# Moving one group's key and query transposes from TensorE to the DMA crossbar, with earlier loads and scores

## The chip, the cores and the metric

The kernel runs on one core of a Trainium2 chip. The metric is the device time of one execution in microseconds (us). The core has five engines that run their own instruction streams side by side: TensorE (PE in the profile; its weight loads are PEld), VectorE (DVE), ScalarE (ACT), GpSimd (POOL) and SyncE (SP). SyncE and GpSimd also issue DMA transfers, which sixteen DMA engines carry out.

## The reference

Sliding-window attention with sink tokens, then a gated feed-forward block:

```python
def _attn_ref(q, k, v, n_sink, window):          # q, k, v: (4, 8, 768, 64) float32
    scores = scale * np.matmul(q, k.transpose(0, 1, 3, 2))
    keep = is_sink | in_window                   # n_sink = 4, window = 128
    scores = np.where(keep, scores, -1000000000.0)
    a = softmax(scores)
    return np.matmul(a, v)

def _moe_ref(x, w_gate, w_val, w_out):           # x: (3072, 512), d_ff = 1536
    g = x @ w_gate
    return (g * sigmoid(g) * (x @ w_val)) @ w_out
```

The attention output of 4 batches, 768 positions, 8 heads of 64 becomes x with 3072 rows of 512.

## The kernel before

**Groups and token blocks.** Attention works on 12 groups of 256 positions, three for each batch; group 3 is the first group of batch 1, group 4 the second. The feed-forward part works on eight token blocks of 256, 256, 256, 512, 512, 512, 512 and 256 tokens. Block 2 is fed by group 2, block 3 by groups 3 and 4.

**One group's chain.** The rows of k and q are loaded (`load_nat`, line 106, four loads of 128 KB, issued by GpSimd and cast to bf16 on the way). They have to be turned so that the head dimension lies on partitions. There are two ways in the code: `step_TN` (line 273) does it on TensorE, four matmuls against an identity for each of four tiles, with an eviction from PSUM (L283 or L285) after each tile; `xbar` (line 287) has SyncE issue four DMA transposes that pass the crossbar, straight from the loaded rows to kT and qT, with no work for a compute engine. Then come the scores (`step_S1`, L382, six PSUM banks; three exponentials on ScalarE at L395), three more exponentials (`step_S2`), masks on VectorE at L404 (`step_S2`, `step_S3`), four steps of probabilities times values (`step_PV`, L494, normalized at L503 and L511), and two steps that turn the output into feed-forward input (`step_X`; from group 3 on a DMA transpose on SyncE, L538).

**Order.** The schedule is written out by hand; each engine executes its instructions in program order. The attention work is woven into a list of feed-forward units (`weave`, line 719): a slot `(14, steps)` puts the steps into unit 14. In the first list, units 12 to 17 are the gates of token block 2 (each two projections, pg and pv, 16 matmuls of 256 columns); units 18 to 23 are `down` units, 12 matmuls of 512 columns each, for blocks 0, 1 and 2. In a gate unit a step marked `ahead` (as `S1` is) runs before the gate's first projection, the others between the two projections. In a down unit with n steps they are spread evenly over the 12 matmuls. A second list follows with block 3, whose first unit holds the scores of group 5.

**Banks.** All PSUM tiles come from one pool of eight banks in rotation; scores take six of them.

**Queues.** GpSimd issues the weight loads (`load_gate`, `load_out`) and the k, q and v loads in program order. The order of loads before the first list is written at lines 803 to 814: gates, group 2's rows, more gates, then four parts of the output weights (384 KB each in bf16), then group 3's rows and values. After these GpSimd clears the tile `vcl` (line 815) and SyncE loads the sink values into it (`load_sinks`, eight small loads, L211). All rows from group 4 on share a single buffer (`natp`), so the rows of the next group are loaded only when the crossbar has read the previous ones. `behind` and `turned` (lines 701 and 705) are one-element copies that make GpSimd wait for a transpose.

Of the kernel before, what the change touches and what calls it, by code (L numbers as in the profile page):

```python
# [14 lines left out]
def kernel(  # L15
# [90 lines left out]
    def load_nat(g):  # L106
        b, c = divmod(g, GC)
        x = (natp if g > 3 else rowp).tile(
            [P, 2, 2, DM], BF16, tag="nat" if g > 3 else "rows", name="nat")
        for i, src in ((0, k), (1, q)):  # L110
            for j in range(2):
                t0 = c * 256 + j * P
                nc.gpsimd.dma_start(  # L113
                    x[:, i, j].rearrange("p (h d) -> p h d", d=D),
                    src[b, :, t0:t0 + P].rearrange("h p d -> p h d"))
        nats[g] = x
# [3 lines left out]
    def load_vm(g):  # L120

        b, c = divmod(g, GC)
        if b not in vms:
            vms[b] = vpool.tile([P, 6, H, VS], BF16, tag=f"vm{b}", name="vm")
            nc.gpsimd.memset(vms[b][:, :, :, D:D + 1], 1.0)

        def part(t, p0, p1, t0):
            nc.gpsimd.dma_start(  # L128
                vms[b][p0:p1, t - 1, :, 0:D],
                v[b, :, t0:t0 + p1 - p0].rearrange("h p d -> p h d"))  # L130

        T = 2 * c
        if g - 1 not in QG:
            part(T - 1, 0, 64, P * (T - 1))
            part(T, 0, P, P * T - 64)
        part(T + 1, 0, 64, P * (T + 1))
        part(T + 1, 64, P, P * (T + 1) - 64)
        if c == GC - 1:
            part(T + 2, 0, 64, P * (T + 2) - 64)
        else:  # L140
            part(T + 2, 0, P, P * (T + 2) - 64)

    def load_v(g):
        if g in QG:
            return load_vm(g)
        b, c = divmod(g, GC)
        va = vpool.tile([P, 2, H, VS], BF16, tag=f"va{g}", name="va")
        nc.vector.memset(va[:, :, :, D:D + 1], 1.0)
        for j in range(2):
            t0 = c * 256 + j * P  # L150
            nc.gpsimd.dma_start(  # L151
                va[:, j, :, 0:D], v[b, :, t0:t0 + P].rearrange("h p d -> p h d"))
        vas[g] = va
# [3 lines left out]
    def load_gate(i, which=(0, 1)):  # L157
        f0, n = sum(FCH[:i]) * P, FCH[i] * P
        both = (wgs, moe_w_gate, "wg"), (wvs, moe_w_val, "wv")
        for lst, w, nm in (both[x] for x in which):  # L160
            t = wpool.tile([P, DMC, n], BF16, tag=f"{nm}{i}", name=nm)
            nc.gpsimd.dma_start(
                t, w[:, f0:f0 + n].rearrange("(c p) f -> p c f", p=P))
            lst.append(t)

    def load_out(i):
        n = DFC // 4
        t = wpool.tile([P, n, DM], BF16, tag=f"wo{i}", name="wo")
        nc.gpsimd.dma_start(
            t, moe_w_out[i * n * P:(i + 1) * n * P].rearrange("(c p) f -> p c f", p=P))  # L170
        wos.append(t)
# [12 lines left out]
    one = const.tile([P, 1], FP32)  # L184
# [62 lines left out]
    def new_T(b):  # L247
        if b not in kTs:
            kTs[b] = kqtp.tile([P, NP2, S], BF16, tag="kT", name="kT")
            qTs[b] = kqtp.tile([P, NP2, S], BF16, tag="qT", name="qT")  # L250
# [36 lines left out]
    def xbar(g, which=(0, 1)):  # L287
        b, c = divmod(g, GC)
        new_T(b)
        for i in which:  # L290
            for j in range(2):
                t0 = c * 256 + j * P
                nc.sync.dma_start_transpose(
                    (kTs, qTs)[i][b][:, :, t0:t0 + P], nats[g][:, i, j])
# [378 lines left out]
    def A(fn, *a):  # L673
        return lambda: fn(*a)

    def TN(g, evict="av"):
        return [A(step_TN, g, i, j, evict) for j in range(2) for i in range(2)]
# [4 lines left out]
    def S1(g, apart=False):  # L682
        f = A(step_S1, g, apart)
        f.ahead = True
        return f

    def one(at, g, apart=False):
        return [(at, [S1(g, apart), A(step_S2, g, apart)]), (at + 1, [A(step_S3, g)])]
# [6 lines left out]
    def PVs(g):  # L695
        return [A(step_PV, g, j, hh) for hh in range(2) for j in range(2)]

    def Xs(g):
        return [A(step_X, g, j) for j in range(2)]
# [108 lines left out]
    load_v(2)  # L808
    load_gate(4)
    load_gate(5)  # L810
    for i in range(4):
        load_out(i)
    load_nat(3)
    load_v(3)
    nc.gpsimd.memset(vcl, 0.0)
    nc.gpsimd.memset(vcl[:, :, D:D + 1], 1.0)
    load_sinks(vcl, 1, B)
# [33 lines left out]
    def L(*fs):  # L851
        def f():
            for x in fs:
                x()
        return f

    def NV(g):
        return L(A(load_nat, g), A(load_v, g))
# [3 lines left out]
        ((8, 8), PVs(2)[:2]), (9, [A(step_PV, 2, 0, 1, "a"), A(step_PV, 2, 1, 1, "a")]),  # L862
        ((10, 11), [A(step_X, 2, 0, "a"), ahead(A(step_X, 2, 1, "a"))]),
        (11, [NV(4), lambda: nc.gpsimd.tensor_copy(out=vcl[64:128], in_=vcl[0:64])]),
        ((14, 14, 15, 15), TN(3, "aa")),
        (15, [A(xbar, 4)]), (15, [A(load_nat, 5)]), (19, [A(xbar, 5, (0,))]),
        *one(17, 3), (18, [A(step_ks, 1)]), (18, [A(step_vsb, 1)]),
        ((19, 19, 19, 20), PVs(3)), (19, [S1(4)]), (20, [L(A(step_S2, 4), A(step_S3, 4))]), (20, Xs(3)), (20, [A(xbar, 5, (1,))]),
        ((21, 21, 21, 22), PVs(4)), (21, Xs(4)[:1]),
        (22, [Xs(4)[1], flush, A(behind, 3, 511), A(load_v, 5), A(load_nat, 6)]),  # L870
        (23, [A(xbar, 6), A(turned, 6), A(load_v, 6), NV(7)])))

    def pair(ga, gb, at=0):
# [51 lines left out]
```

## Time and profile before

| What | Value |
|---|---|
| Median of 3 runs | 233.2 us (233.0 to 233.44) |
| Profiled execution | 233.82 us |
| Its span, first to last instruction | 231.9 us |
| Mean granted TensorE clock | 0.993 |
| VectorE, ScalarE, GpSimd busy | 65%, 46%, 36% |
| Loads on the GpSimd queue (q0) | 79904 packets, 14.29 MB |
| SyncE queue (q1) | 30672 packets, 11.58 MB |

The DMA traffic in 40 slices of the span, as busy tenths of the DMA engines:

```profile
DMA  8999999999998998998989996989915102000132
```

The page lists for each engine how long it was busy, and for each group of instructions how many there were, how long one took, and what ended the engine's idle time before them. TensorE's busy time counts pipelined matmuls whose ends are modelled, so the starts of instructions are the better measure of its pace. The tile view of a DMA issue tells how long it took from issue to landing. The DMA view of a time window counts the packets that each queue moved in it.

### The profile page before, as it was taken

The numbers are of one execution on the slowest core, as the hardware profiler recorded it, in microseconds if no ns is written. First come the engines' busy times: TensorE is split into PE (matmuls) and PEld (weight loads), VectorE is DVE, ScalarE is ACT, GpSimd is POOL, SyncE is SP. The second block draws the span as 40 slices with busy tenths as digits, with TensorE's granted clock in tenths as the row PEclk, the third lists the DMA queues.
The fourth block names the chain that finished last, engine by engine and source line by source line (L and its number), as shares of the span: only waits on it lengthen the run. The fifth ranks groups of instructions, "written<-read, shape, count | busy, mean of one in ns | idle before, by whom it ended". The sixth has DMA issues, their size and how long they took to land.

```text
span 231.9 us, 5433 instructions
## 1 busy us (share of the span) xinstructions
PE 225.6 (97%) x2155; PEld 125.4 (54%) x2155; DVE 150.9 (65%) x327; ACT 106.4 (46%) x212; POOL 84.3 (36%) x123
## 2 busy tenths in 40 slices
PE   7699999999999999999999999999999999999994
PEld 3469645796555644455444454454454544487443
DVE  5878888767660797960797970597960599778000
ACT  4784486566543726423635512835612823333221
POOL 8996874960500907806353415135000000000000
PEclk9979999999999999999999999999999999999999
DMA  8999999999998998998989996989915102000132
GB/s 147 150 185 179 179 198 206 164 156 122 123 154 230 103 134 99 151 195 141 146 119 139 128 124 138 105 109 144 117 40 144 45 3 42 3 3 0 64 120 90
DMA packets 112008, 28.04 MB, mean 121 GB/s; under 512 B 99056, under 2 KB 109040, under 8 KB 111984
## 3 DMA queue, kind: packets, MB, share of 16 engines
q0 software_dynamic: 79904, 14.29, 80.7%
q1 hardware_dynamic: 30672, 11.58, 26.7%
q10 hardware_dynamic: 1408, 1.84, 2.5%
q8 instruction: 17, 0.28, 0.5%
q14 instruction: 7, 0.06, 0.1%
HBM read 29.13 MB, written 6.29 MB: 153 GB/s over the span
## 4 chain that ended last, share of the span: by engine, by line
PE 94%; DMA 2%; POOL 2%; DVE 0%; issue 0%; POOLq 0%
PE pg L564 27%; PE pv L564 27%; PE pd L657 27%; PE o L494 4%; PE s L382 3%; DMA rows<-in_q_dram 2%; PE s L326 1%; PE o L463 1%; PE pk L432 1%; PE pn L279 1%; PE o L454 1%; POOL rows L102 1%; POOL x L216 1%; PE px L543 1%; DVE xT L550 0%
## 5 line engine op out<-in xcount | busy, mean ns | idle before, releaser
L592 DVE SCALAR_TENSOR_TENSOR u<-th,pg 128x512 bf16<-128x512 f32 x72 | 49.2, 683 | 45.4 <-ACT th L584 45.1
L564 PE MATMUL pg<-xT,wg 128*128 128x512 bf16 (+1 forms) x360 | 74.2, 337 | 0.3 <-DVE xT L550 0.3
L564 PE MATMUL pv<-xT,wv 128*128 128x512 bf16 (+1 forms) x360 | 74.1, 336 | 0.0
L584 ACT ACTIVATE th<-pg 128x512 f32<-128x512 f32 x72 | 43.7, 608 | 59.6 <-PE pg L564 59.6
L657 PE MATMUL pd<-wo,ht 128*128 128x512 bf16 (+2 forms) x300 | 65.9, 370 | 0.0
L564 PEld LDWEIGHTS <-wg 128*128 128x128 bf16 x360 | 34.4, 98 | 26.7 <-issue 0.7
L564 PEld LDWEIGHTS <-wv 128*128 128x128 bf16 x360 | 33.9, 98 | 23.5 <-issue 0.2
L607 DVE TENSOR_TENSOR ht<-u,pv 128x512 bf16<-128x512 bf16 x62 | 42.5, 686 | 4.7 <-PE pv L564 0.4
L657 PEld LDWEIGHTS <-ht 128*128 128x128 bf16 x300 | 27.5, 98 | 28.4
L662 ACT ACTIVATE ot<-pd 128x512 f32<-128x512 f32 (+1 forms) x24 | 14.3, 595 | 50.2 <-PE pd L657 46.8
L395 ACT ACTIVATE e<-s 128x512 bf16<-128x512 f32 x54 | 28.5, 614 | 5.8 <-PE s L382 4.9
L113 POOL DMA_DIRECT2D nat<-in_k_dram x20 | 17.7, 895 | 29.3 <-DMA qT<-nat 27.8
L511 DVE TENSOR_TENSOR xn<-o,rcp 128x256 bf16<-128x256 f32 x45 | 17.9, 419 | 0.7
L128 POOL DMA_DIRECT2D vm<-in_v_dram x24 | 17.8, 770 | 1.2 <-DMA va<-in_v_dram 0.7
L113 POOL DMA_DIRECT2D nat<-in_q_dram x20 | 17.8, 906 | 1.0 <-DMA wv<-in_moe_w_val_dram 0.5
L494 PEld LDWEIGHTS <-e 128*128 128x128 bf16 x256 | 12.0, 100 | 6.3 <-issue 0.3
L404 DVE TENSOR_TENSOR e<-e,maskq 128x768 bf16<-128x768 bf16 x24 | 13.1, 553 | 1.9 <-ACT e L395 1.9
L151 POOL DMA_DIRECT2D va<-in_v_dram x12 | 10.7, 917 | 4.3 <-DMA wo<-in_moe_w_out_dram 2.4
L703 POOL CAST warmed<-xT 1x1 f32<-1x1 bf16 x3 | 0.5, 175 | 30.2 <-DMA xT<-xn 30.2
L503 DVE RECIPROCAL rcp<-o 128x4 f32<-128x4 f32 x48 | 7.3, 172 | 5.5 <-PE o L494 5.3
L664 DVE TENSOR_SCALAR ot<-pd 128x128 f32<-128x128 f32 x1 | 0.3, 292 | 14.3 <-PE pd L657 14.3
L333 ACT ACTIVATE e<-s 128x512 bf16<-128x512 f32 x16 | 8.3, 607 | 0.6 <-PE s L326 0.5
(86 smaller groups left out, 138.7 us busy)
## 6 DMA issues: line engine op xcount, KB each, us to landing
out_dram<-ot SPq DMA_DIRECT2D x17, 256.0 KB
nat<-in_k_dram POOLq DMA_DIRECT2D x20, 128.0 KB, 4.7
nat<-in_q_dram POOLq DMA_DIRECT2D x20, 128.0 KB, 4.9
va<-in_v_dram POOLq DMA_DIRECT2D x12, 128.0 KB, 5.9
wg<-in_moe_w_gate_dram POOLq DMA_DIRECT2D x6, 256.0 KB, 7.6
wv<-in_moe_w_val_dram POOLq DMA_DIRECT2D x6, 256.0 KB, 8.2
wo<-in_moe_w_out_dram POOLq DMA_DIRECT2D x4, 384.0 KB, 11.1
out_dram<-ot ACTq DMA_DIRECT2D x6, 256.0 KB
```

Of the source, the lines that this page charges most:

```text
L113: nc.gpsimd.dma_start(x[:, i, j].rearrange("p (h d) -> p h d", d=D), src[b, :, t0:t0 + P].rearrange("h p d -> p h d"))
L128: nc.gpsimd.dma_start(vms[b][p0:p1, t - 1, :, 0:D], v[b, :, t0:t0 + p1 - p0].rearrange("h p d -> p h d"))
L395: nc.scalar.activation(e_t[g][:, e0:e0 + 512], pss[g][w, i], AF.Exp, scale=scale)
L404: nc.vector.tensor_tensor(e, e, m.broadcast_to([P, 2, 384]), op=ALU.mult)
L494: nc.tensor.matmul(o, l, r, start=(c == 0 and i == 0), stop=(i == len(mms) - 1), skip_group_check=True)
L511: nc.vector.tensor_tensor(xn, po[:, :, 0:D], rcp.broadcast_to([P, 4, D]), op=ALU.mult)
L564: nc.tensor.matmul(ps[:, i * n:(i + 1) * n], ws[fi][:, c, fo * P:(fo + 1) * P], xTs[tb][:, c], start=(c == 0), stop=(c == DMC - 1))
L584: nc.scalar.activation(th, pg, AF.Tanh, scale=0.5)
L592: nc.vector.scalar_tensor_tensor(u, th, 1.0, pg, op0=ALU.add, op1=ALU.mult)
L607: nc.vector.tensor_tensor(hts[tb][:, f:f + 512 // SIZES[tb]].rearrange("p a n -> p (a n)"), u, pv, op=ALU.mult)
L657: nc.tensor.matmul(po, hts[tb][:, f, ts * P:(ts + 1) * P], wos[f // n][:, f % n, lo:hi], start=(f == 0), stop=(f == DFC - 1))
L662: nc.scalar.activation(ot, po, AF.Copy, scale=0.5)
```

## The change

Group 3's keys and queries are turned by four crossbar transposes instead of 16 matmuls and four evictions. Its rows are loaded ahead of the output weights, its values between the second and the third part of them. The crossbar transposes are issued on SyncE ahead of the sink-value loads. Group 3's scores go from unit 17 to unit 14, its value steps from the down units 19 and 20 to the gates 16 and 17, its output transposes from unit 20 to unit 18. Group 4's scores go from unit 19 to 20, its second step from 20 to 21, its value steps from 21 and 22 to 22 and 23. The crossbar transposes of group 5, before split over units 19 and 20, stand together in unit 20. The issue of group 5's values and group 6's rows goes from unit 22 to 23.

```diff
     load_gate(5)
-    for i in range(4):
-        load_out(i)
     load_nat(3)
+    load_out(0)
+    load_out(1)
     load_v(3)
+    load_out(2)
+    load_out(3)
+    xbar(3)
     nc.gpsimd.memset(vcl, 0.0)
...
-        ((14, 14, 15, 15), TN(3, "aa")),
-        (15, [A(xbar, 4)]), (15, [A(load_nat, 5)]), (19, [A(xbar, 5, (0,))]),
-        *one(17, 3), (18, [A(step_ks, 1)]), (18, [A(step_vsb, 1)]),
-        ((19, 19, 19, 20), PVs(3)), (19, [S1(4)]), (20, [L(A(step_S2, 4), A(step_S3, 4))]), (20, Xs(3)), (20, [A(xbar, 5, (1,))]),
-        ((21, 21, 21, 22), PVs(4)), (21, Xs(4)[:1]),
-        (22, [Xs(4)[1], flush, A(behind, 3, 511), A(load_v, 5), A(load_nat, 6)]),
+        *one(14, 3), (15, [A(xbar, 4)]), (15, [A(load_nat, 5)]),
+        ((16, 16, 17, 17), PVs(3)), (18, [A(step_ks, 1)]), (18, [A(step_vsb, 1)]), (18, Xs(3)),
+        (20, [S1(4)]), (20, [A(xbar, 5)]), (21, [L(A(step_S2, 4), A(step_S3, 4))]),
+        ((22, 22, 22, 23), PVs(4)), (22, Xs(4)[:1]),
+        (23, [Xs(4)[1], flush, A(behind, 3, 511), A(load_v, 5), A(load_nat, 6)]),
```

`one(at, g)` puts `step_S1` and `step_S2` of group g into unit `at` and `step_S3` into the next.

## The prediction

> **What bounds the kernel now.** I read the page first, then TensorE's timeline around the change, then the queues of SyncE and GpSimd, then the DMA traffic.
>
> ```profile
> PE 225.6 (97%) x2155; PEld 125.4 (54%) x2155; DVE 150.9 (65%) x327; ACT 106.4 (46%) x212; POOL 84.3 (36%) x123
> PE 94%; DMA 2%; POOL 2%; DVE 0%; issue 0%; POOLq 0%
> ```
>
> The second line, from the chain that ended last, gives TensorE 94% of the span. So the time changes in two ways only: TensorE gets less to do, or it gets something to wait for. TensorE's timeline around the touched units (start, duration, instruction):
>
> ```profile
> 46.21 1.04 PE L564 MATMUL pg<-xT,wg 128*128 128x256 bf16 x8
> 47.09 0.61 PE L279 MATMUL pn<-ident,nat 128*128 128x128 bf16 x8
> 47.53 1.04 PE L564 MATMUL pv<-xT,wv 128*128 128x256 bf16 x8
> ...
> 49.28 0.61 PE L279 MATMUL pn<-ident,nat 128*128 128x128 bf16 x8
> 49.73 1.04 PE L564 MATMUL pv<-xT,wv 128*128 128x256 bf16 x8
> ...
> 52.44 0.84 PE L382 MATMUL s<-qT,kT 64*128 64x256 bf16 x18
> 53.21 1.05 PE L564 MATMUL pg<-xT,wg 128*128 128x256 bf16 x8
> ```
>
> Durations overlap, so I go by starts. Unit 14 begins at 46.21; group 3's transposes take 47.09 to 47.53 and 49.28 to 49.73; its scores come at 52.44. No idle time is marked before any row here.
>
> **What is removed.** 16 transposes: 0.44 + 0.45 = 0.89 us of TensorE, all on the bounding engine. ScalarE also loses four evictions (L283, 0.58 to 0.60 us) and waits on TensorE before and after them anyway: nothing.
>
> **What is moved without price, if its data are there.** The scores of group 3 (0.77 us) and its four value steps (0.13 + 0.24 + 0.12 + 0.25 = 0.74 us by starts at 58.42 to 62.47) only change places. Their chain must still fit. From the start of the scores, by the rows after 52.44, the last of the first three exponentials ends at +2.0, tanh at +2.5, the next three end at +4.0. VectorE then alternates u (0.69, less overlap), mask (0.55), ht (0.69): the second mask ends near +4.8, the fourth near +6.9. TensorE reaches the first value step at 0.77 + 0.89 + 4 x 0.87 = +5.15 and the third at about +7.3. Slack 0.4 us at both: hidden, and were it not, the price is what VectorE is late. Group 4's scores, by unit lengths (12 x 0.217 us for a `down`), come at 54.97 - 0.89 + 0.74 + 28 x 0.217 = 60.9 instead of 60.30.
>
> **What is added: four transposes through the crossbar, early.** Scores of group 3 now stand at the head of unit 14, so TensorE needs all four at 46.2 instead of the untransposed rows at 47.1. When can they be there? GpSimd's queue holds at most eight loads in flight; a ninth waits for the eighth before it:
>
> ```profile
> 27.11 0.75 POOL L169 DMA_DIRECT2D wo<-in_moe_w_out_dram  x1 [0.38 <-DMA wg<-in_moe_w_gate_dram]
> ...
> 31.48 0.91 POOL L113 DMA_DIRECT2D nat<-in_k_dram  x1 [0.57 <-DMA wg<-in_moe_w_gate_dram]
> ```
>
> The loads of group 3 take the places at 27.1 to 31.1. Loads land in order behind a backlog, as the landing of the last gate load and of the first of group 3's shows:
>
> ```profile
> L162 POOL DMA_DIRECT2D wv<-in_moe_w_val_dram x1: 780/780/780, 25.9 to 25.9; - x1
> DMA to landing us min/median/max: 9.3/9.3/9.3
> ...
> L113 POOL DMA_DIRECT2D nat<-in_k_dram x1: 909/909/909, 31.5 to 31.5; - x1
> DMA to landing us min/median/max: 12.3/12.3/12.3
> ```
>
> The gate load lands at 25.95 + 9.3 = 35.25. Group 3's four landed at 43.8, 44.7, 45.65 and 46.5 behind four output loads, 0.9 to 1.0 us apart; moved ahead they land at about 36.2, 37.2, 38.1 and 39.1. SyncE has been idle since its first loads, so it issues the first transpose at 36.3. Its instruction takes 1.25 us, but the data move later, and slower under load:
>
> ```profile
> 40.87 2.67 SPq L211 DMA_DIRECT2D vcl<-in_v_dram  x8
> 49.81 2.59 SPq L293 DMA_TRANSPOSE kT<-nat  x2
> ...
> q0 software_dynamic: 1220, 0.15, 249.7%
> ...
> q0 software_dynamic: 2343, 0.29, 263.4%
> q1 hardware_dynamic: 544, 0.13, 26.8%
> ...
> q0 software_dynamic: 1108, 0.14, 121.5%
> q1 hardware_dynamic: 537, 0.13, 69.7%
> ...
> q1 hardware_dynamic: 1069, 0.26, 127.3%
> ```
>
> The q lines are packets, MB and share in four stretches. 50:51: loads alone, 1220 packets a us. 51.4:54.6 and 124.8:126.7: the first transpose of group 4 and of group 9, beside loads; one transpose is 544 packets, and transposes follow one another. 55.3:56.3: no loads left, two transposes in 1.0 us. The same count for the first transposes of groups 7, 8, 10 and 11 gives 2.2, 1.75, 2.45 and 1.86 us. So one transpose costs 0.5 us alone and (3.2 + 2.2 + 1.75 + 1.9 + 2.45 + 1.86) / 6 = 2.2 us beside a full load queue. Its first packet comes 1.6 to 2.4 us after the issue, mean 2.1.
>
> Between 36 and 55 us the load queue is full without a break, so I take 2.2: 36.3 + 2.1 + 4 x 2.2 = 47.2. The release follows the last packet by about 1.1 us (group 4: last packets near 56.4, GpSimd released at 57.48). Group 3's scores start at 48.3, not 46.2: **a new wait of 2.1 us**. Queued behind it on TensorE is everything; ScalarE and VectorE have no backlog and wait with it.
>
> The duration beside 1 KB output-weight packets is not in this trace (nearest rows: loads of 128-byte packets). Bounds: 0.5 us each as when alone, then the last issue (40.2) decides, all is there by 43, and the wait is 0; and 3.2 us each, the worst row, 38.4 + 12.8 + 1.1 = 52.3, a wait of 6.1.
>
> [...]
>
> **What the transposes do to the loads.** In the six stretches the loads moved 1108 to 2343 packets where 1220 a us would have been 2135 to 3904: about 1.0 us lost for each transpose, 4 in all. Output weights then land by 53 at the latest, first needed at 54.8 (parts 2 and 3 from 56.1): hidden. Values of group 3 land by 49, needed after 51: hidden. The eight small `vcl` loads now stand behind the transposes on SyncE, and the last four wait for their landings: about 50, needed after 54.8: hidden. Group 4's loads land at about 53.9, its transposes at 57.2 + 4.0 = 61.2; its scores come at 60.9 + 2.1: hidden by the first wait, and worth 0.3 us without it. The transposes of group 5 likewise move with group 4's. In return SyncE is freer for group 4's outputs, which finish no later relative to unit 23.
>
> **Sum.** The profiled execution took 233.82 us (231.9 span, 1.9 around it): 233.82 - 0.89 + 2.1 = 235.0. It lies 0.6 above the median of the runs, 233.2, so the forecast is **234.4 us**. About 0.2%, 0.47 us, is what a measurement of this kernel tells from no change.
>
> **Rivals.**
> A, no wait. The transposes pass quickly beside large packets (about 1.7 us each suffices: 36.3 + 2.1 + 6.8 + 1.1 = 46.3). For it: the second transposes of groups 7 and 9, 1.4 to 1.5 us beside a thinner queue. Against: 3.2 us for group 4. Then 233.2 - 0.89 = 232.3, or 232.6 with 0.3 us at group 4.
>
> B, output weights starve the crossbar. If a transpose must let 1108 load packets pass whatever their size, the 768 packets of two output loads take 3.7 us (832 came in 36 to 40). Walking the queue from 38.4, with 0.5 us for each transpose's own packets, gives 41.0, 44.2, 45.6 and 50.1; released at 51.2, a wait of 5.0: 237.3. It decides from the point where a transpose takes over 2.7 us.
>
> C, late at group 4. Group 3 is in time, but the backlog of 4 us makes group 4's transposes, loaded themselves, end 1 to 2 us after 60.9: 233.2 - 0.89 + 1.5 = 233.8. Against it: 3 us of slack today, and the unlisted last transposes of that group run alone.
>
> **How the numbers follow.** Forecast (wait 1.4 to 3.5) 0.37, A 0.34, B 0.17, C 0.12. The likeliest alone covers 233.7 to 235.8; taking in the ends, 0 and 6.1 us of wait, the range is 232.3 to 238.3. Faster is A, nearly whole: 0.33. Within 0.2% is the edge of A, half of C and a bit of the forecast: 0.15. Slower: 0.52.
>
> **What will show it.** Right: L279 falls from 32 transposes to 16; the first kT transpose is issued on SyncE near 36.3; TensorE idles before L382's s, released by the DMA of qT, about 2 us; and unit 18 starts about 2 us later than 54.8. Wrong: s of group 3 starts at 46.2 to 46.6 (A), after 50.5 (B), or the idle time stands before group 4's or 5's scores (C). It would also be wrong if the loads of group 3 landed well off 36 to 39 us, or if value steps at units 16 and 17 waited for masks.

## The result, and the profile after

| | Median | Lowest to highest | Ratio to before (95%) |
|---|---|---|---|
| before (6 runs) | 233.25 us | 233.0 to 235.19 | 1 |
| after (6 runs) | 244.15 us | 240.17 to 245.79 | 1.034 [1.0247, 1.0432] |

The change makes the kernel slower by 3.4%. The direction had the larger chance in the forecast (0.52). The size was far off: 234.4 us with a range up to 238.3 was forecast. The ratio is formed from the shorter of the runs after (240.17 and 242.81). The profiled execution took 244.24 us with a span of 242.4, so about 3 us of what its trace shows are not in the ratio.

The page of the changed kernel, in the lines that answer to those of before: TensorE's busy time, the chain that ended last, and TensorE and its granted clock in 40 slices of 6.06 us.

```profile
PE   7789999508999999999999999999999999999994
PEclk9999999955999999999999999999999999999999
...
PE 73%; DMA 15%; POOL 4%; DVE 3%; issue 2%; SPq 2%; DVEq 0%; POOLq 0%
```

TensorE's share of the chain fell from 94% to 73%, and DMA's rose from 2% to 15%. Two things stand next to each other in the slices: slices 8 and 9 (42.4 to 54.5 us) are half empty and empty, and in slices 9 and 10 (48.5 to 60.6 us) the clock is about half. Before had no such slice after the first three:

```profile
PEclk9979999999999999999999999999999999999999
```

TensorE's timeline in the changed kernel (start, duration, instruction, idle time before it and what ended it):

```profile
44.53 1.04 PE L564 MATMUL pv<-xT,wv 128*128 128x256 bf16 x8
55.45 1.47 PE L382 MATMUL s<-qT,kT 64*128 64x256 bf16 x18 [9.89 <-DMA qT<-nat]
56.85 1.89 PE L564 MATMUL pg<-xT,wg 128*128 128x256 bf16 x8
58.53 1.53 PE L564 MATMUL pv<-xT,wv 128*128 128x256 bf16 x8
59.90 1.04 PE L564 MATMUL pg<-xT,wg 128*128 128x256 bf16 x8
...
72.00 0.89 PE L382 MATMUL s<-qT,kT 64*64 64x192 bf16 x52
83.85 0.89 PE L382 MATMUL s<-qT,kT 64*64 64x192 bf16 x52
```

The wait is where the forecast put it, before group 3's scores, and the crossbar's transpose of the queries ends it. It lasts 9.89 us instead of 2.1. The next rows show the second cost: by starts the scores take 1.40 us instead of 0.77, and the two projections 1.68 and 1.37 instead of 0.87 each. At 59.90 the pace is normal again. The windows view of the two stretches gives length, then busy time and count for TensorE, its weight loads, VectorE, ScalarE and GpSimd, then the granted clock, the DMA share and GB/s:

```profile
45.50:55.40 9.90, 0.06 (x1) 0.00 (x0) 1.23 (x2) 0.00 (x0) 0.69 (x1) 0.69 2.04 125
55.40:60.00 4.60, 4.55 (x35) 3.40 (x36) 0.59 (x1) 2.80 (x6) 2.57 (x4) 0.55 2.24 127
```

In the wait TensorE stands still and nearly only DMA works (VectorE 1.23 us, GpSimd 0.69). In the second stretch the clock is 0.55. The trace's clock records show half speed from 49.29 to 59.53 us, so 59.53 - 55.45 = 4.1 us of work at half speed, about 2.0 us of loss.

**A measure for comparisons.** The first 20 us differ between executions by up to 2.2 us, whatever the kernel (in the profiled ones half clock lasted 3.41 us there in before, 6.83 in one variant, and did not occur in after). So below I compare the stretch from the first gate of unit 4 (before: 24.73) to group 5's scores (before: 73.68), which holds all that the change touches:

| Kernel | Stretch, us | Against before |
|---|---|---|
| before | 73.68 - 24.73 = 48.95 | |
| after | 83.85 - 23.91 = 59.94 | +10.99 |

The terms close: 9.89 (wait) + 1.99 (clock, the remainder, beside 2.0 by the records) - 0.89 (transposes saved) = 10.99. The spans differ by 242.4 - 231.9 = 10.5: the start was 0.82 us earlier in this execution, and the rest after group 5's scores 0.33 longer.

**Where the wait comes from.** SyncE's queue in the changed kernel:

```profile
36.65 2.77 SPq L293 DMA_TRANSPOSE kT<-nat  x2
39.51 2.79 SPq L293 DMA_TRANSPOSE qT<-nat  x2
42.39 13.19 SPq L211 DMA_DIRECT2D vcl<-in_v_dram  x8
```

The first issue is 0.35 us later than forecast, so the rows came in time. By the packet records the first packet moved at 40.59, and the four transposes ended at 43.01, 46.46, 50.80 and 53.68: 2.42, 3.45, 4.34 and 2.88 us, 13.1 in all. The DMA view of this stretch (40.6 to 53.7 us; packets, MB, share):

```profile
q0 software_dynamic: 3467, 1.11, 144.9%
q1 hardware_dynamic: 2176, 0.52, 55.8%
```

2176 packets are the four transposes at 544 each. In 13.1 us both queues together moved 1.63 MB, 124 KB a us. This is the lowest rate of the stretches below, so the transposes did not simply give way to loads: both were slow. For 0.7 us of the third transpose (49.8 to 50.5 us) they nearly stood still:

```profile
q1 hardware_dynamic: 14, 0.00, 30.5%
q0 software_dynamic: 12, 0.01, 25.8%
```

### The profile page after: what moved, and what is told of

Its sections match the earlier page's. It is cut to its first block, busy times and chain, and to the rows that moved or that the text cites. A ratio compares the mean times of both kernels' runs of the same rounds, so it can differ in the third digit from the quotient of the medians.

```text
span 242.4 us, 5384 instructions
## 1 busy us (share of the span) xinstructions
PE 224.2 (93%) x2113; PEld 124.9 (52%) x2139; DVE 150.4 (62%) x327; ACT 104.6 (43%) x208; POOL 84.9 (35%) x123
## 4 chain that ended last, share of the span: by engine, by line
PE 73%; DMA 15%; POOL 4%; DVE 3%; issue 2%; SPq 2%; DVEq 0%; POOLq 0%
PE pd L657 25%; PE pg L564 21%; PE pv L564 20%; DMA qT<-nat 6%; DMA nat<-in_k_dram 4%; PE s L382 3%; DMA wg<-in_moe_w_gate_dram 3%; PE o L494 2%; DMA x<-in_q_dram 2%; SPq L293 2%; POOL nat L113 1%; POOL wv L162 1%; PE o L463 1%; DVE ht L607 1%; DVE u L592 1%
## 5 line engine op out<-in xcount | busy, mean ns | idle before, releaser
L592 DVE SCALAR_TENSOR_TENSOR u<-th,pg 128x512 bf16<-128x512 f32 x72 | 49.1, 682 | 52.4 <-ACT th L584 52.2
L657 PE MATMUL pd<-wo,ht 128*128 128x512 bf16 (+2 forms) x289 | 63.9, 370 | 0.7 <-issue 0.2
L395 ACT ACTIVATE e<-s 128x512 bf16<-128x512 f32 x54 | 28.5, 614 | 14.2 <-PE s L382 13.3
L404 DVE TENSOR_TENSOR e<-e,maskq 128x768 bf16<-128x768 bf16 x24 | 13.1, 551 | 7.4 <-ACT e L395 7.4
L382 PE MATMUL s<-qT,kT 64*64 64x64 bf16 (+4 forms) x366 | 8.5, 223 | 9.9 <-DMA qT<-nat 9.9
L494 PEld LDWEIGHTS <-e 128*128 128x128 bf16 x256 | 11.3, 98 | 5.2 <-issue 0.2
L382 PEld LDWEIGHTS <-kT 64*64 64x64 bf16 (+1 forms) x366 | 6.8, 108 | 13.6 <-issue 12.7
```

The source lines that it names most:

```text
L382: nc.tensor.matmul(pss[g][w, lo // 8][part, 64 * (lo % 8):64 * (lo % 8) + 64 * (hi - lo)], kTs[b][r, p, k0:k0 + kn], qTs[b][r, p, cc:cc + ...
L395: nc.scalar.activation(e_t[g][:, e0:e0 + 512], pss[g][w, i], AF.Exp, scale=scale)
L494: nc.tensor.matmul(o, l, r, start=(c == 0 and i == 0), stop=(i == len(mms) - 1), skip_group_check=True)
L592: nc.vector.scalar_tensor_tensor(u, th, 1.0, pg, op0=ALU.add, op1=ALU.mult)
L657: nc.tensor.matmul(po, hts[tb][:, f, ts * P:(ts + 1) * P], wos[f // n][:, f % n, lo:hi], start=(f == 0), stop=(f == DFC - 1))
```

## The experiments

My theory after the result: the crossbar is late because of the loads beside it, and the wait, being long, costs the clock as well. Rivals: the moved steps and loads cost time by themselves; loads and transposes pass packet for packet, so that packet size decides; the load queue has no room for four more transposes at any place. "Stretch" is the measure above.

**1. The schedule without the crossbar.** Loads, scores and all other moves as in the change, but group 3's transposes back on TensorE, in unit 12:

```diff
-    xbar(3)
...
-        *one(14, 3), (15, [A(xbar, 4)]), (15, [A(load_nat, 5)]),
+        ((12, 12, 12, 12), TN(3, "aa")), *one(14, 3), (15, [A(xbar, 4)]), (15, [A(load_nat, 5)]),
```

> The changed order of loads and of the woven steps, but group 3 is turned on TensorE (16 transposes in unit 12, evicted by ScalarE) and not by the crossbar. If the crossbar's lateness is the whole loss, TensorE idles less than 0.5 us before group 3's scores, the clock stays whole after the start, and the time is that of the kernel before, 232.8 to 234.0 us. If the early scores in the gates, the later group 4 or the late output weights cost something by themselves, it stays above 235 us.

Measured: 234.43 us, ratio 1.003 [1.0009, 1.0052], stretch 48.95, the same as before to the hundredth. The moved loads, scores and value steps cost nothing in the stretch; the loss comes with the crossbar. The 0.3% of the total lie outside the stretch: in the profiled execution 0.32 us of it stand ahead of unit 4. Why was not followed up.

**2. The clock's price.** 36 idle matmuls on zeros keep TensorE busy during the wait:

```diff
+        if g == 3:
+            fill(36, bank([P, 512], FP32, "w"), 512)
```

> The changed kernel with 36 matmuls on a zero tile (36 x 0.217 = 7.8 us) put on TensorE just ahead of group 3's scores; their result is used by nobody. If the half clock from 49.3 to 59.5 us comes from the idle time, it is gone: scores and the projections behind them take 2.5 us, not 4.5, and the time falls by about 2.0 us against the changed kernel, to 242 us where that takes 244. If the clock fell for another reason, nothing changes. The scores' own start, 55.4 us, moves by less than 1 us in both.

Measured: 243.32 us, 1.0418 [1.0355, 1.0482]; stretch 55.82 (+6.87). TensorE's timeline:

```profile
47.52 7.93 PE L732 MATMUL w<-zero 128*128 128x512 bf16 x35
55.38 0.84 PE L384 MATMUL s<-qT,kT 64*128 64x256 bf16 x18
56.15 1.05 PE L566 MATMUL pg<-xT,wg 128*128 128x256 bf16 x8
```

After the filled wait the scores take 0.84 us and not 1.47, and no half clock is recorded there. From group 3's to group 5's scores it takes 26.48 us, against 28.40 in the change: 1.92 us is the clock's price. The scores' own start says nothing here: the idle matmuls themselves end at 55.45 us, and no wait for the transposes is left behind them. The total did not fall. The profiled execution was 2 us later at unit 4, with half clock until 17.57; so only the time between the two scores shows the price.

**3. Transposes alone, weights behind them.** All output weights wait on GpSimd until the last transpose (first variant) or only the first one (second) has landed:

```diff
     load_nat(3)
     load_v(3)
     xbar(3)
+    turned(3)
     for i in range(4):
         load_out(i)
```

In the second variant this stands in place of `turned(3)`:

```diff
+    nc.gpsimd.tensor_copy(out=warmed[0:1], in_=kTs[1][0:1, 0, 127:128])
```

> The changed kernel, but the four output-weight loads (and all loads after them) are issued only when group 3's four crossbar transposes have landed; group 3's rows and values come ahead of them. If the loads beside the crossbar are what makes it late (both theories of it), the transposes need 0.5 to 2 us each, end by 44 us, TensorE does not idle before group 3's scores, and the time is 232.3 to 234 us, unless the output weights then come late for unit 18, which would show as idle time before pd. If the crossbar is late for a reason of its own, the wait stays at 5 us or more and the time above 238 us.

> As the run that held the output weights until all four transposes had landed, but they are held only until the first has landed, 1.9 us earlier by that run's trace. The weights' data need 2.7 us from issue to first packet, by which time the other three are through. Group 3's scores should not wait. Group 4's scores, which waited 3.4 us there, should wait about 1.5 us, with no half clock behind them: 233.7 - 0.9 + 1.5 = 234.3 us. If the load queue's lost time isn't what made group 4 late, the wait stays at 3.4 us and the time at 237 to 239 us.

Measured: 238.58 us, 1.0197 [1.0143, 1.0251], and 237.22 us, 1.0151 [1.0125, 1.0178]; stretches 52.80 (+3.85) and 52.17 (+3.22). With the loads gone, the transposes of the first variant ran in 1.45, 0.56, 0.57 and 0.84 us, the first of them still beside the last loads. The DMA view of the first variant from 38.4 to 41.9 us:

```profile
q1 hardware_dynamic: 2174, 0.52, 97.5%
q0 software_dynamic: 794, 0.10, 44.8%
```

The same 2174 packets that took 13.1 us in the change take 3.5 here. Group 3's scores start at 45.51 and 46.18 without a wait. But both expectations missed: a new wait stands before group 4's scores. First variant, then second:

```profile
63.61 1.50 PE L382 MATMUL s<-qT,kT 64*64 64x192 bf16 x52 [3.40 <-DMA qT<-nat]
```

```profile
63.23 0.89 PE L382 MATMUL s<-qT,kT 64*64 64x192 bf16 x52 [2.35 <-DMA qT<-nat]
```

Holding the weights left the load queue empty for 4.4 and 2.8 us, and GpSimd issued everything behind them later: group 4's rows at 47.59 and 46.60 us, 42.45 before. Their transposes were issued at 55.26 and 54.35, 49.81 before. Both variants also show half clock for 3.41 us at or soon after this wait: in the first group 4's scores took 1.50 us, not 0.89; in the second the 22 output matmuls behind them took 6.61 us, against 4.92 in the second kernel of experiment 4.

**4. What stands beside the transposes.** Three kernels set other loads beside them. One puts all weights, 1 KB packets, behind the rows; one puts the weights last, behind group 4's rows and values, which move in 128-byte packets; one is the kernel before with only its transposes changed, late, beside small packets too:

```diff
     load_nat(3)
+    for i in range(4):
+        load_out(i)
     load_v(3)
     xbar(3)
```

```diff
     load_nat(3)
     load_v(3)
+    load_nat(4)
+    load_v(4)
     for i in range(4):
         load_out(i)
     xbar(3)
```

```diff
     load_v(3)
...
     load_sinks(vcl, 1, B)
+    xbar(3)
...
-        ((14, 14, 15, 15), TN(3, "aa")),
```

> The changed kernel with all four output-weight loads straight behind group 3's rows and group 3's values behind them, so that the crossbar runs beside 1 KB packets alone. If packet size is what slows it, a transpose takes 3.3 us or more and group 3's scores start at 55 to 60 us; the time is 244 us or more. If the mixture of row, value and weight loads is what slows it, a transpose is quicker than in the changed kernel and the scores start before 53 us.

> The changed kernel with group 3's values and group 4's rows and values loaded ahead of the output weights, so that the crossbar runs at the same time and behind the same eight loads, but beside 128-byte packets. If packet size slows it: 1.9 us a transpose as in the crossbar with the old load order, first packet 2.1 to 3 us after the issue, so the scores start at 36.5 + 2.6 + 7.6 + 1.4 = 48 us, a wait of 2.5 to 3 us and no half clock before them. If the depth of the load queue slows it: scores at 55 us as in the changed kernel. The output weights come late for unit 18 here, 4 us or more, so the whole time says nothing on this.

> The kernel before with its order of loads and its slots, but group 3 is turned by the crossbar, issued on SyncE behind the sink-value loads; scores stay in unit 17. The rows land from 43.8 us on, behind the output weights, so the transposes run beside 128-byte loads alone. If 1 KB weight packets are what slows the crossbar, a transpose takes about 2.2 us as in the rows of before: 46 + 8.8 + 1.1 = 55.9, against 51.6 for the scores, a wait of 4.3 and 236.5 us. If any full load queue slows it as much as in the changed kernel (3.3 us and 3.9 to the first packet), the scores start at 61, a wait of 9 or more and over 241 us.

| Transposes beside | Median, ratio | Issue to first packet | Each, us | Wait | Stretch |
|---|---|---|---|---|---|
| weights first | 240.81, 1.0306 [1.0265, 1.0347] | 3.9 | 3.41, 2.62, 2.77, 1.29 | 5.88 | +7.57 |
| rows and values | 237.24, 1.0182 [1.0131, 1.0232] | 3.46 | 2.30, 1.58, 1.60, 1.54 | 2.51 | +1.68 |
| kernel before, late | 242.49, 1.0375 [1.0331, 1.0419] | 2.95 | 2.76, 1.62, 1.52, 1.45 | 6.51 | +7.72 |
| the change | 244.15, 1.034 [1.0247, 1.0432] | 3.94 | 2.42, 3.45, 4.34, 2.88 | 9.89 | +10.99 |

TensorE's rows in the first two, and the DMA view of the second from 39.6 to 47 us:

```profile
51.52 1.47 PE L382 MATMUL s<-qT,kT 64*128 64x256 bf16 x18 [5.88 <-DMA qT<-nat]
```

```profile
48.32 0.84 PE L382 MATMUL s<-qT,kT 64*128 64x256 bf16 x18 [2.51 <-DMA qT<-nat]
```

```profile
q0 software_dynamic: 4813, 0.61, 130.1%
q1 hardware_dynamic: 2176, 0.52, 59.8%
```

Wait and stretch are those of one execution for each kernel, and these are not alike: the one of "rows and values" took 235.23 us, 2 us less than its median, the one of the change 244.24, some 3 us more than its shorter runs.

Beside rows and values the four transposes and 0.61 MB of loads pass in 7.4 us, 153 KB a us; in the change it was 124. There the wait shrinks to 2.5 us, and the profile shows no half clock after it (the scores take 0.84 us). So the neighbour decides. That the mixture of weights and values in the change is worse than weights first is not shown: the shorter runs of the change (240.17 and 242.81) stand against 240.67 and 240.94, and in the kernel of experiment 2, which has the loads and transposes of the change, the four took 2.24, 1.83, 2.54 and 4.16 us, 10.8 in all, against 10.1 in "weights first" and 13.1 in the profiled execution of the change.

How the neighbour acts can be read within "weights first". The DMA view from 41 to 44 us, beside 1 KB packets, and from 49.1 to 50.6 us, beside 128-byte packets:

```profile
q0 software_dynamic: 479, 0.47, 91.8%
q1 hardware_dynamic: 481, 0.12, 30.1%
...
q0 software_dynamic: 636, 0.08, 80.9%
q1 hardware_dynamic: 636, 0.15, 80.2%
```

In both stretches the two queues move equal numbers of packets, whatever the size: about 160 each in a us beside the large ones, 424 beside the small ones. So in these stretches loads and transposes pass packet for packet, and the transpose is slower beside the larger packets: the first took 3.41 us, the last 1.29. By what rule the packets take their places, the counts do not show. Nor are they the whole account. The third transpose took 2.77 us though 508 of the 537 load packets beside it were small, as both queues nearly stood still from 48.2 to 49 us:

```profile
q1 hardware_dynamic: 43, 0.01, 18.7%
q0 software_dynamic: 42, 0.01, 10.4%
```

Why they stand still there, as in the change, is not settled. And over four transposes the numbers are not equal: beside rows and values 4813 load packets went by beside their 2176, in the change 3467.

The third kernel was expected between a cheap and a dear crossbar. The transposes took 1.45 to 2.76 us each, about what the cheap theory said. But the first was issued at 46.60 us, after SyncE had waited 2.2 us for the sink-value loads, and its first packet moved at 49.55, where the expectation had 46; half clock came on top (by starts the scores took 1.40 us and the two projections 1.68 and 1.48, as in the change).

The weights of the second kernel landed at 52.2 to 58.0 us and TensorE did not wait for them, against the expectation.

**5. Half of the transposes.** Only the keys pass the crossbar, the queries stay on TensorE in unit 12; first in the order of the change, then in the order of the second kernel of experiment 4 (group 4's loads ahead of the weights). And a third kernel: that order with all four transposes, but the scores only in unit 16:

```diff
-    xbar(3)
+    xbar(3, (0,))
...
-        *one(14, 3), (15, [A(xbar, 4)]), (15, [A(load_nat, 5)]),
+        ((12, 12), TN(3, "aa")[1::2]), *one(14, 3), (15, [A(xbar, 4)]), (15, [A(load_nat, 5)]),
```

```diff
-        *one(14, 3), (15, [A(xbar, 4)]), (15, [A(load_nat, 5)]),
-        ((16, 16, 17, 17), PVs(3)), (18, [A(step_ks, 1)]), (18, [A(step_vsb, 1)]), (18, Xs(3)),
+        *one(16, 3), (15, [A(xbar, 4)]), (15, [A(load_nat, 5)]),
+        ((18, 18, 18, 19), PVs(3)), (18, [A(step_ks, 1)]), (18, [A(step_vsb, 1)]), (19, Xs(3)),
```

> The changed kernel, but only group 3's keys go through the crossbar (two transposes); its queries are turned on TensorE in unit 12. By 2.4 to 3.4 us a transpose beside weights the keys land at 40.6 + 5.9 + 1.4 = 47.9 us: a wait of about 2.4 us, too short for the half clock, so 233.7 - 0.45 + 2.4 = 235.6 us, against 244 with four. If the loss doesn't grow with the number of transposes (a fixed start-up of the crossbar), the time stays above 240 us.

> The same load order with group 3's scores in unit 14, but only its keys go through the crossbar and its queries are turned on TensorE: 0.45 us less for TensorE than before, half the added DMA time. The keys land at 36.2 + 3.4 + 2 x 1.76 + 1.3 = 44.4 us, before unit 14, so the scores don't wait. If the room in the load stream decides, two transposes fit better than four: stretch from unit 4 to group 5's scores 48.5 to 49.0 us, time 233.0 to 233.7 us, a tie with before. If each added transpose is paid anyway, 49.5 us or more.

> The run that loads group 3's and group 4's rows and values ahead of the output weights, with group 3's scores two units later (unit 16, values in the down units 18 and 19), past the landing of its transposes at 48.2 us. The wait of 2.5 us before those scores goes. If the transposes' DMA time is really hidden then, the stretch from unit 4 to group 5's scores is 48.95 - 0.89 = 48.1 us, and the time beats the kernel before, about 232.8 to 233.0 us. If the load stream as a whole has no room for four more transposes, idle time of 1 to 2 us comes up again behind it (before the last quarter of the output weights in unit 18, or before group 4's or 5's scores), the stretch is 49 to 50 us, and the time 233.5 to 235 us.

Measured: 236.37 us, 1.0123 [1.009, 1.0156]; 235.41 us, 1.008 [1.0034, 1.0126]; 236.22 us, 1.0116 [1.0077, 1.0154]. Stretches 49.93 (+0.98), 51.33 (+2.38) and 52.57 (+3.62). With two transposes group 3's scores no longer wait in either profile. That 236.37 lies near the expected 235.6 is luck: the wait that the expectation was made of did not come, and the profiled execution took 234.58. That a wait of 2.4 us is too short for the half clock, no run shows: one of 2.35 us (experiment 3) had it soon after, those of 2.51 (experiment 4) and 2.52 us (the second kernel here) had none. In all three the largest wait is elsewhere, before group 5's scores: 1.35, 2.52 and 1.89 us. The third also waits 0.64 us at group 3's scores, 0.73 us for masks and 0.72 us for weights. The second kernel, first TensorE, then GpSimd:

```profile
75.33 0.89 PE L382 MATMUL s<-qT,kT 64*64 64x192 bf16 x52 [2.52 <-DMA qT<-nat]
```

```profile
61.77 1.77 POOL L113 DMA_DIRECT2D nat<-in_k_dram  x2 [5.93 <-issue]
```

Up to here I read this as a load queue without room. The GpSimd row says something else: group 5's rows are issued at 61.77 us by an engine that has stood idle for 5.93 us. In the kernel before it stood idle too, until 57.48, and the row names a crossbar transpose:

```profile
57.48 1.75 POOL L113 DMA_DIRECT2D nat<-in_k_dram  x2 [6.13 <-DMA qT<-nat]
```

All rows from group 4 on share one buffer, and group 4's last transpose releases it (the third kernel's trace names the DMA of qT at this place). So a delay of group 4's transposes passes on to group 5's rows, and from there to its scores.

**6. Another buffer for group 5's rows.** They go to one of the three buffers of the earlier groups, and group 4's first transpose releases their loads instead of its last. Tried on the second and the first kernel of experiment 5:

```diff
-        x = (natp if g > 3 else rowp).tile(
+        x = (natp if g > 3 and g != 5 else rowp).tile(
...
-(15, [A(load_nat, 5)])
+(15, [lambda: nc.gpsimd.tensor_copy(out=warmed[0:1], in_=kTs[1][0:1, 0, 383:384]), A(load_nat, 5)])
```

> The kernel of e10 (group 4's loads ahead of the output weights, only group 3's keys through the crossbar), with group 5's rows in one of the three buffers of the earlier groups and their loads released by the landing of group 4's first transpose instead of its last. In e10 TensorE idled once, 2.52 us before group 5's scores: group 5's rows were issued at 61.77 us, when the fourth transpose of group 4 had freed the shared buffer. Theory 'shared buffer': the issue comes near 57.7, 4 us earlier, the idle time goes, the stretch from unit 4 to group 5's scores falls from 51.33 to about 48.9 us, and the kernel stands at 233.0 to 233.7. Theory 'no room in the load stream': the earlier rows only collide with group 4's transposes, a wait of 1 us or more appears before group 4's or group 5's scores, and it stays above 234.5.

> The kernel of e8 (the change with only group 3's keys through the crossbar, its queries on TensorE), with the same two edits: group 5's rows in a buffer of the earlier groups, released by group 4's first transpose. In e8 the only idle time was 1.35 us before group 5's scores, its rows issued at 61.08 us. Theory 'shared buffer': issue near 57.2, no idle time, stretch 48.6 us (0.44 us of TensorE's transposes saved), 0.1% to 0.2% below the kernel before, 233.0 to 233.6. Theory 'no room': a wait of 1 us or more before group 4's or 5's scores, 234.5 or above.

Measured: 233.84 us, 1.0006 [0.9987, 1.0024], and 234.8 us, 1.0028 [0.9998, 1.0058]; stretches 48.65 (-0.30) and 50.33 (+1.38). GpSimd and TensorE of the first:

```profile
58.31 0.18 POOL L868 CAST warmed<-kT 1x1 f32<-1x1 bf16 x1 [2.84 <-DMA kT<-nat]
59.20 1.78 POOL L113 DMA_DIRECT2D nat<-in_k_dram  x2 [0.71 <-issue]
```

```profile
60.62 0.89 PE L382 MATMUL s<-qT,kT 64*64 64x192 bf16 x52
72.47 0.89 PE L382 MATMUL s<-qT,kT 64*64 64x192 bf16 x52
```

The issue comes 2.6 us earlier (4 were expected), and no wait is left before group 4's or group 5's scores. The theory of the shared buffer holds, and "no room in the load stream" falls for two transposes: 235.41 becomes 233.84 us. With four transposes the second buffer was not tried. That is not measurably different from before: the 0.44 us of TensorE that two transposes save show as 0.30 in the stretch. The second kernel lost its wait at group 5 too, but in its profiled execution the keys of group 3 came late:

```profile
47.89 0.73 PE L382 MATMUL s<-qT,kT 64*128 64x128 bf16 x16 [1.45 <-DMA kT<-nat]
```

The same instructions up to there gave no wait in the first kernel of experiment 5. So the time that the crossbar needs among these loads also varies from execution to execution by more than a microsecond. No version tried is measurably faster than the kernel before.

## Why the prediction was wrong, point by point

**The step that failed** is "36.3 + 2.1 + 4 x 2.2 = 47.2. The release follows the last packet by about 1.1 us", which gave "a new wait of 2.1 us". Term by term, against this execution:

| Term | Forecast | Measured |
|---|---|---|
| Scores wanted | 46.2 | 45.5 |
| First issue | 36.3 | 36.65 |
| Issue to first packet | 2.1 | 3.94 |
| Four transposes | 8.8 | 13.1 |
| Last packet to scores | 1.1 | 1.77 |
| Scores start | 48.3 | 55.45 |

The first issue was right. Two terms were mis-sized, and in the kernel of experiment 2, with the same loads and transposes, too: 4.03 us to the first packet and 10.8 for the four. The first is the latency: I averaged transposes issued when the load queue was thinning out (1.6 to 2.4 us); with a full queue it is 2.95 to 3.94 in four kernels. The second is the transpose itself: 3.3 us on average instead of 2.2. The bound from the worst row (3.2 us) was exceeded: two of the four took 3.45 and 4.34. The rows had been transposes beside 128-byte loads only. Experiment 4 shows that beside such loads 1.8 us is right, and that beside weights it is not. The prediction said that this case is not in the trace, and still closed the range with the worst row of the other case. (By its own terms the range ends at 233.2 - 0.89 + 6.1 = 238.4, not 238.3.)

**A term left out: the clock.** The wait of 9.89 us was followed by half clock until 59.53, 1.9 to 2.0 us more (experiment 2). The trace of before had half clock of 3.41 us in its start phase (11.42 to 14.84 us), where TensorE's longest single wait is 1.2 us: that the clock can fall was there to be read, what a long wait does to it was not. The lengths of half clock in these runs are 3.41, 6.83 and 10.24 us, one, two and three times the same. What sets them, no run shows; the wait of 2.35 us in experiment 3 is shorter than the shortest of them and had half clock soon after it all the same.

**"Loads lose 4 us"** became 9.5. The first of group 4's rows landed at 59.4 us, forecast 53.9, of which 4 us were that loss: 2.4 us for each transpose and not 1.0. The long wait covered it; with a shorter wait it would have shown, as in experiments 3 and 5, where the wait stands before group 4 or group 5.

**What was right.** Removed work, 0.89 us: with the clock's price from its records, 2.04, the sum of the stretch is 11.04 against 10.99. Moved steps for nothing: experiment 1. Place and releaser of the wait: the trace. The weights were not waited for: the trace.

**The rivals.** A (no wait) fell. B ("output weights starve the crossbar", 0.17) had the side and the place, scores after 50.5, but half the price (5.0 us of wait). Its mechanism, load packets counted whatever their size, is in part what experiment 4 shows, but at one load packet for one of the transpose, not 1108 for its 544. Beside 1 KB packets alone one transpose took 3.41 us; the 4.34 us of the change's third hold the standstill of 0.7 us. C (late at group 4) did not decide here, but is what the kernels of experiment 3 ran into once group 3 was in time.

**What stays open.** Why both queues together nearly stand still for 0.7 to 0.8 us, and are slow in the change at other times too; and why the loss varies so that six runs of the same kernel lie between 240.17 and 245.79 us. The wait of 9.89 us is that of a long execution; in the shorter runs, some 3 us shorter as a whole, it was probably less by about as much, by estimate from the total times.

## What to carry to other kernels

Here the transposes moved off TensorE paid with the load queue: 16 matmuls of 0.89 us were exchanged for transfers of 3.5 us with the loads held back and 10.8 and 13.1 among the change's loads. Before trusting the price of such a move, ask which loads fly beside it, and take the latency from a place where the queue is as full as it will be there (here 1.6 to 2.4 us from issue to first packet where the queue thinned out, 2.95 to 4.03 where it was full). When a wait has been removed and the time does not come back, look at the next users of the same buffer before calling the queue full: an issuing engine that stands idle (5.93 us at GpSimd here) and issues later than before (61.77 us against 57.48) was here the sign of a held buffer and not of a lack of bandwidth.

## What the hardware showed that was not expected

- Four transposes of 128 KB took 3.5 us with the loads held back, 7.0 and 7.4 beside small packets, 10.1 in "weights first", and 13.1 and 10.8 in two executions beside weights and values; in the one of 13.1 the two queues together also moved less (124 KB a us, against 153 and 177).
- The three longest waits that were not filled, 5.88, 6.51 and 9.89 us, had half clock after them (scores of 1.46 or 1.47 us, not 0.84). Of the waits of 2.35 to 3.40 us, those of 2.35 and 3.40 had half clock for 3.41 us at or soon after them, those of 2.51 and 2.52 none.
- In two stretches of "weights first" loads and transposes moved equal numbers of packets, whether the loads' packets had 1 KB (479 and 481 in 3 us) or 128 bytes (636 and 636 in 1.5 us).
